# SyncE's order of loads in the opening of a clustered attention and gated feed-forward kernel

## The chip, the cores and the metric

One core of one Trainium2 chip. The metric is the device time of one execution in microseconds (us); 299.18 us is the median of three runs of the kernel before (298.58 to 301.35). SyncE issues most of the transfers, GpSimd the weights' loads and the later values; TensorE, ScalarE, VectorE and GpSimd compute.

## The reference

Attention in which a query sees only the keys of its own cluster, and then a gated feed-forward layer without a gate matrix:

```python
def _attn_ref(q, k, v, centroids):            # q, k, v: (4, 8, 768, 64); centroids: (8, 16, 64)
    q_assign = argmax(einsum('bhsd,hcd->bhsc', q_n, c_n))      # nearest of 16 normalised centroids
    k_assign = argmax(einsum('bhsd,hcd->bhsc', k_n, c_n))
    mask = q_assign[:, :, :, None] == k_assign[:, :, None, :]
    scores = where(mask, scale * q @ k.T, -1e9)
    return softmax(scores) @ v

def _moe_ref(x, w_in, w_out):                 # x: (3072, 512), d_ff 2048
    h = x @ w_in
    return (h * sigmoid(h)) @ w_out
```

## The kernel before

**Jobs.** The rows of queries and keys come in jobs of 128 partitions by up to 12 pieces of 64. Jobs k0 to k7 hold batch 0's keys of one head and the first half of its queries; x0 and x1 hold the second halves of batch 0's queries for four heads each (the extra queries); h8 to h31 hold queries and keys of one head of batches 1 to 3. A job is loaded (`load`), split into a high and a low half in f16 (`hi`, `lo`, lines 123 to 132), transposed (on TensorE with `tr` in the opening, by a DMA transpose, `xpose`, line 141, later), multiplied with the centroids (`psN`, line 180), and the one-hot of the nearest cluster becomes 16 further rows of the transposed tile `ab`, the codes. In the opening `cd_ev` takes the codes out of PSUM and SyncE copies them into `ab` by a small transfer (line 261: "code transfer", 40 or 48 KB). With the codes in the contraction a score of unlike clusters comes out so low that its exponential vanishes.

**Score units.** A unit (`qk`, line 354, then `ex` on ScalarE, line 359) is two key tiles by 384 queries. The first 24 units are the first query halves of batch 0's heads 0 to 7, three units a head: units 0 to 2 need job k0, 3 to 5 k1, 6 to 8 k2, 12 to 14 k4. Each pair of heads then gets its products with the values (`pO`, line 371), is normalised and transposed into `xt`, and the feed-forward units (`ph`, line 421, tanh and gate) and the second matrix (`po`, lines 480 and 561) follow.

**Order.** The scheduling is by hand: an engine runs its instructions in the order in which the program issues them. The opening, up to score unit 26, is written out word by word in `plan`: `vl1` loads the values of head 1, `v1` casts them on GpSimd, `r8` loads job h8 (two transfers of 192 KB, queries and keys), `xr0` loads x0 (one of 384 KB), `xh0` and `xl0` split it, `ce1` to `ce7` take out a job's codes and issue their transfer, `w0` to `w11` load weights from GpSimd. Behind the opening a small planner takes over: each engine has a lane of pieces with the time from which they can run, and picks the one whose due time (ready plus `late`) is first. `load_v` and `cast_v` are the values' load and cast there; five buffers `vn` hold values between load and cast. All that SyncE issues goes in one order, a wait of one transfer holding back those behind it.

Of the kernel before, what the change touches and what calls it, by code (L numbers as in the profile page):

```python
# [34 lines left out]
def kernel(  # L35
# [11 lines left out]
    B, H, S, D = q.shape  # L47
# [240 lines left out]
    def load_v(i, eng=nc.sync):  # L288
        vn = mp.tile([128, NJ, D], f32, name="vn", bufs=5)
        eng.dma_start(vn.rearrange("p j d -> p (j d)"), v[i // H, i % H].rearrange("(p j) d -> p (j d)", j=NJ))  # L290
        vns[i] = vn
# [397 lines left out]
    def first(op, n, eng, banks):  # L689
# [93 lines left out]

    plan = """
        hk0 hq0 hi1.A lk0 cn0 lq0 lo1 tk0.0 hi2.A evk0.D j3.1 c5.12 kad tq0.3 lo2 evq0.A tr1.23 stk vl4 L0.0 vl0
        evq1.A evk1.D mx0 ge0 hi4.A tr2.13 evq2.A L1.2 hi3.P ct0.03 lo4 mx1 ge1 xr0 cm1 ctk0 hi5.P evk2.A lo5 ctq0
        tr4.10 ce1.A qk0 hi7.P evk4.A lo3 L2.3 evq4.A tr5.21 mx2 evk5.D ge2 qk1 ex0 qk2 evq5.A w0 lo7 L4.0 vl1 ex1 mx4
        cm2 tr3.12 ex2 ce2.A xr1 qk3 evq3.D evk3.A qk4 hi6.P tr7.32 ge4 lo6 cm4 L3.1 evq7.D xh0.P ex3 qk5 vl2 evk7.D
        ce4.A v4 mx3 w1 ex4 tr6.20 evk6.D ex5 L5.3 ge3 mx5 vl5 qk6 v1 evq6.A ct3.21 vl3 ge5 qk7 cm5 L6.0 xl0 ctk3 ex6
        ctq3 qk8 ce5.A L7.S.2 xq0.3 mx6 ge6 ls7 xp0.1 xw0.D v0 xh1.P w2 ex7 cm6 v2 v5 qk9 ex8 ce6.A qk10 ex9 pa0.3 mx7  # L790
        ge7 pb0 vl6 xu0.D xl1 qk11 xL0.0 ex10 cm7 vl7 qk12 v3 ex11 xM0 ce7.D xs0 w3 pc0 v7 qk13 r8 xp1.1 ex12 qk14 xm0
        ex13 xu1.D ex14 w4 xq1.2 qk15 xg0 v6 nm0 pa1.1 qk16 xw1.D xc0 pt0.3 ex15 xe0.D ex16 qk17 ex17 xL1.2 w5 pb1
        qk18 vl8 ex18 xM1 qk19 pe0.D pc1 qk20 nm1 vl9 xs1 pa2.0 ex19 ex20 qk21 pb2 qk22 ex21 pc2 xm1 xg1 ex22 nm2 w6
        qk23 px3.3 pt1.1 pe1.D ex23 pt2.0 xc1 py3 qk24 pe2.D w7 r9 xe1.A r10 nm3 ex24 qk25 a0.1 pt3.0 w8 qk26 a1.2
# [38 lines left out]
    def lands(t, work, rest):  # L833
        nonlocal moves_end
        moves_end = max(t, moves_end) + work
        return moves_end + rest

    def add(eng, ready, length, f, then=None, late=0.0):
        lanes[eng].append((ready, ready + late, length, f, then))
# [120 lines left out]
    def value_free(i, t):  # L960
        if i - 5 not in cast_at:
            after_cast[i - 5] = lambda t: value_free(i, t)
            return
        t = max(t, cast_at[i - 5] + 0.06)
        if i >= 2 * H:
            add("POOL", t, 0.6, lambda: load_v(i, nc.gpsimd), lambda t: got_v(i, t))
        else:
            add("SP", t, 0.7, lambda: load_v(i), lambda t: got_v(i, t))

    def got_v(i, t):  # L970
        values_at[i] = lands(t, 0.78, 1.0)
        if i in waiting:
            waiting.pop(i)(t)
# [18 lines left out]
    for i in range(H, B * H):  # L992
        b, h = divmod(i, H)
        p = SPLIT[i - H]
        job = jobs[i]
        if i > H + 3:
            date(p - AHEAD[b - 1], lambda t, i=i: raw_free(i, t))
        if i >= H + 2:
            date(p - VALUES[b - 1], lambda t, i=i: value_free(i, t))
        date(p, chain(job, b))  # L1000
        date(p + CAST[b - 1], lambda t, i=i: cast(i, t))
# [305 lines left out]
    while True:  # L1307
# [11 lines left out]
        t, e, piece = best  # L1319
# [34 lines left out]
```

## Time and profile before

| | |
|---|---|
| median of 3 runs | 299.18 us (298.58 to 301.35) |
| profiled execution | 297.6 us, its span 295.8 us |
| TensorE busy | 288.1 us of the span (97%) |
| ScalarE, VectorE, GpSimd busy | 222.0, 219.3, 73.4 us |
| granted TensorE clock | 0.999 |
| transfers | 44.61 MB, mean 151 GB/s |

The times in the views are in us from the start of the span. A line such as "19.60 0.81 ACT L359" gives start, length, engine and the line of the kernel; in square brackets stands how long the engine had been idle before it, and what ended that. A line "ab<-cd SPq DMA_DIRECT2D x1, 40.0 KB, 3.9" is a transfer issued by SyncE, its size and the time from issue to landing. PE is TensorE, PEld its loading of weights, ACT ScalarE, DVE VectorE, POOL GpSimd, SP SyncE.

### The profile page before, as it was taken

To read this page: it belongs to the slowest core of one execution; us is meant where nothing else is said; L and a number is where in the kernel's file an instruction comes from. 1 tells how busy PE (TensorE), PEld (TensorE's weight loads), DVE (VectorE), ACT (ScalarE), POOL (GpSimd) and SP (SyncE) were. 2 spreads that over 40 slices of the span, in tenths; PEclk is the share of its full clock that TensorE was granted. 3 is DMA by queue.
4 is the path that set the end of the run, shared out by engine and by line. 5 is a ranking of instruction groups with operands and counts; after the bars stand their busy time and mean duration, and the time that the engine had idled before them with its cause. 6 is when DMAs were issued, how large, how long until landed. Compare 5 with 4: busy or idle time off the path is not lost.

```text
span 295.8 us, 8187 instructions
## 1 busy us (share of the span) xinstructions
PE 288.1 (97%) x3273; PEld 203.5 (69%) x3273; DVE 219.3 (74%) x459; ACT 222.0 (75%) x365; POOL 73.4 (25%) x133
## 2 busy tenths in 40 slices
PE   7899999999999999999999999999999999999995
PEld 3777766666765566667766776778767786767783
DVE  5999679496997799997797676997664644569743
ACT  5899889655896679987579668997798879744410
POOL 2985700002050023652332540252300000000000
PEclk9999999999999999999999999999999999999999
DMA  7888999999866499989987979796210020110013
GB/s 216 249 175 187 204 256 196 182 264 204 233 139 182 110 227 224 230 195 206 219 174 147 188 218 228 175 122 126 73 50 17 13 86 16 49 38 0 35 38 142
DMA packets 77220, 44.61 MB, mean 151 GB/s; under 512 B 56288, under 2 KB 73088, under 8 KB 77184
## 3 DMA queue, kind: packets, MB, share of 16 engines
q1 hardware_dynamic: 71952, 35.55, 52.0%
q0 software_dynamic: 4800, 8.13, 14.6%
q8 instruction: 25, 0.41, 0.6%
q10 hardware_dynamic: 432, 0.43, 0.4%
q14 instruction: 11, 0.09, 0.1%
HBM read 27.30 MB, written 6.29 MB: 114 GB/s over the span
## 4 chain that ended last, share of the span: by engine, by line
PE 87%; DMA 5%; ACT 4%; DVE 2%; issue 1%; DVEq 0%; ACTq 0%
PE ph L421 28%; PE pS L354 19%; PE po L561 16%; PE pO L371 10%; PE po L480 8%; PE psN L180 3%; ACT P L359 3%; DMA ab<-hl 2%; DMA ab<-cdt 1%; DVE hl L132 1%; DMA ab<-cd 1%; DMA raw<-in_k_dram 1%; ACT ab L164 0%; PE px L393 0%; PE psC L246 0%
## 5 line engine op out<-in xcount | busy, mean ns | idle before, releaser
L359 ACT ACTIVATE P<-pS 128x768 f16<-128x768 f32 x192 | 156.6, 825 | 34.9 <-PE pS L354 33.9
L421 PE MATMUL ph<-xt,win_s 128*128 128x384 f16 x512 | 97.6, 326 | 0.0
L354 PE MATMUL pS<-ab 128*128 128x384 f16 x384 | 93.3, 326 | 1.0 <-DMA ab<-cd 0.5
L444 DVE SCALAR_TENSOR_TENSOR gt<-tn,ph 128x384 f16<-128x384 f32 x110 | 58.6, 550 | 21.2 <-ACT tn L441 20.5
L421 PEld LDWEIGHTS <-win_s 128*128 128x128 f16 x512 | 49.2, 98 | 31.2
L441 ACT ACTIVATE tn<-ph 128x384 f32<-128x384 f32 x110 | 55.2, 514 | 3.2 <-PE ph L421 2.3
L354 PEld LDWEIGHTS <-ab 128*128 128x128 f16 x384 | 34.4, 98 | 19.7 <-DMA ab<-cd 0.9
L371 PEld LDWEIGHTS <-P 128*128 128x128 f16 x1152 | 39.8, 97 | 4.4
L371 PE MATMUL pO<-vt,P 128*128 128x65 f16 x1152 | 41.2, 193 | 0.0
L561 PEld LDWEIGHTS <-gt 128*128 128x128 f16 x304 | 29.3, 98 | 6.0 <-DVE gt L544 0.4
L132 DVE SCALAR_TENSOR_TENSOR hl<-raw,hl 128x768 f16<-128x768 f32 (+3 forms) x35 | 32.4, 931 | 0.6 <-ACT hl L123 0.3
L480 PE MATMUL po<-wout_s,gt 128*128 128x512 f16 x128 | 32.5, 379 | 0.0
L295 POOL CAST vt<-vn 128x384 f16<-128x384 f32 x32 | 19.2, 607 | 50.7 <-DMA vn<-in_v_dram 38.1
L561 PE MATMUL po<-wout_s,gt 128*128 128x256 f16 x192 | 24.4, 273 | 0.0
L224 POOL TENSOR_SCALAR od<-od 128x96 f16<-128x96 f16 x16 | 10.0, 627 | 57.3 <-DVE od L217 57.2
L180 PEld LDWEIGHTS <-ab 128*128 128x128 f16 x458 | 17.4, 97 | 4.7 <-DMA ab<-hl 0.8
L381 DVE RECIPROCAL zr<-pO 128x6 f32<-128x6 f32 x32 | 6.2, 193 | 19.1 <-PE pO L371 19.0
L480 PEld LDWEIGHTS <-gt 128*128 128x128 f16 x128 | 12.0, 98 | 10.7
L180 PE MATMUL psN<-stk,ab 128*128 128x32 f16 (+1 forms) x458 | 18.6, 188 | 0.6 <-DMA ab<-hl 0.6
L383 DVE TENSOR_TENSOR xn<-pO,zr 128x384 f16<-128x384 f32 x32 | 17.8, 557 | 1.1
L192 DVE TENSOR_REDUCE L<-psN 128x192 f32<-128x384 f32 (+1 forms) x27 | 14.8, 549 | 2.3 <-PE psN L180 2.2
L561 PE MATMUL po<-tw,sg 128*128 128x256 f16 x128 | 16.3, 273 | 0.0
(101 smaller groups left out, 259.1 us busy)
## 6 DMA issues: line engine op xcount, KB each, us to landing
raw<-in_k_dram SPq DMA_DIRECT2D x31, 192.0 KB, 3.8
out_dram<-ot SPq DMA_DIRECT2D x23, 256.0 KB, 2.3
raw<-in_q_dram SPq DMA_DIRECT2D x24, 192.0 KB, 4.1
vn<-in_v_dram SPq DMA_DIRECT2D x16, 192.0 KB, 4.0
vn<-in_v_dram POOLq DMA_DIRECT2D x16, 192.0 KB, 3.5
win_s<-in_moe_w_in_dram POOLq DMA_DIRECT2D x8, 256.0 KB, 6.1
wout_s<-in_moe_w_out_dram POOLq DMA_DIRECT2D x4, 512.0 KB, 19.5
raw<-in_q_dram SPq DMA_DIRECT2D x2, 384.0 KB, 4.7
```

The source lines that it names most:

```text
L132: nc.vector.scalar_tensor_tensor(out=hl[:, s, 1, :], in0=raws[job.name][:, s, :], scalar=QS, in1=hl[:, s, 0, :], op0=ALU.mult, op1=ALU.sub ...
L180: nc.tensor.matmul(L[:, n % g, :, n // g], ab[:, i, :], stk[:, job.groups[i // 3][0], x : x + w], start=(x == 0), stop=(x + w == 2 * HC),)
L295: nc.gpsimd.tensor_copy(vt[:, :, 0:D], vns.pop(i))
L354: nc.tensor.matmul(pS[:, e, 0:HALF], abs_[kj.name][:, kn, :], rhs, start=True, stop=True)
L359: nc.scalar.activation(out=P, in_=pst.pop(u)[:, :, 0:HALF], func=AF.Exp, bias=0.0, scale=ESC)
L371: nc.tensor.matmul(o[:, (2 * t + h) * VW : (2 * t + h + 1) * VW], Ps[i + h, c, j // 2][:, j % 2, ts(t, 128)], vtb[(i + h) % 13][:, j, 0:VW ...
L383: nc.vector.tensor_tensor(out=xn, in0=ov[:, :, 0:D], in1=zr.unsqueeze(2).to_broadcast([128, 2 * NM, D]), op=ALU.mult)
L421: nc.tensor.matmul(ph[:, 0:HALF], win_s[:, r, ts(fb, 128)], xts[b, c][:, r, :], start=(r == 0), stop=(r == NR - 1))
L441: nc.scalar.activation(out=tn, in_=ph[:, 0:HALF], func=AF.Tanh, bias=0.0, scale=1.0)
L444: nc.vector.scalar_tensor_tensor(out=gt[:, fb, :], in0=tn, scalar=1.0, in1=ph[:, 0:HALF], op0=ALU.add, op1=ALU.mult)
L480: nc.tensor.matmul(po, gts[b, c][:, fc, ts(t, 128)], wout_s[:, fc, :], start=(fc == 0), stop=(fc == NFB - 1))
L561: nc.tensor.matmul(o, l[:, f, :], x, start=(f == 0 and k in begins), stop=(f == HK - 1), skip_group_check=True)
```

## The change

Two words of `plan` move, and one argument in the planner. `xr0` moves from ahead of `cm1` to behind `ce1`; `r8` moves from behind `qk13` to behind `vl1`; and a load of values by SyncE for heads 8 to 11 gets 3 us more until it is due.

```diff
-        evq1.A evk1.D mx0 ge0 hi4.A tr2.13 evq2.A L1.2 hi3.P ct0.03 lo4 mx1 ge1 xr0 cm1 ctk0 hi5.P evk2.A lo5 ctq0
-        tr4.10 ce1.A qk0 hi7.P evk4.A lo3 L2.3 evq4.A tr5.21 mx2 evk5.D ge2 qk1 ex0 qk2 evq5.A w0 lo7 L4.0 vl1 ex1 mx4
+        evq1.A evk1.D mx0 ge0 hi4.A tr2.13 evq2.A L1.2 hi3.P ct0.03 lo4 mx1 ge1 cm1 ctk0 hi5.P evk2.A lo5 ctq0
+        tr4.10 ce1.A xr0 qk0 hi7.P evk4.A lo3 L2.3 evq4.A tr5.21 mx2 evk5.D ge2 qk1 ex0 qk2 evq5.A w0 lo7 L4.0 vl1 r8 ex1 mx4
...
-        ge7 pb0 vl6 xu0.D xl1 qk11 xL0.0 ex10 cm7 vl7 qk12 v3 ex11 xM0 ce7.D xs0 w3 pc0 v7 qk13 r8 xp1.1 ex12 qk14 xm0
+        ge7 pb0 vl6 xu0.D xl1 qk11 xL0.0 ex10 cm7 vl7 qk12 v3 ex11 xM0 ce7.D xs0 w3 pc0 v7 qk13 xp1.1 ex12 qk14 xm0
...
-            add("SP", t, 0.7, lambda: load_v(i), lambda t: got_v(i, t))
+            add("SP", t, 0.7, lambda: load_v(i), lambda t: got_v(i, t), 3.0 if i < H + 4 else 0.0)
```

The order of the instructions differs on SyncE alone. In the opening, from behind the last loads of batch 0's rows (`vn` are values; `raw` of 128x4x192 the extra queries, of 128x384 h8's rows; `ab<-cd` the code transfers of k1, k2, k4, k5 and k6), before:

```order
L290 DMA vn<-in_v_dram 128x384 x2
L113 DMA raw<-in_q_dram 128x4x192
L261 DMA ab<-cd 16x5x256
L290 DMA vn<-in_v_dram 128x384
L261 DMA ab<-cd 16x5x256
L113 DMA raw<-in_q_dram 128x4x192
L290 DMA vn<-in_v_dram 128x384
L261 DMA ab<-cd 16x5x256
L290 DMA vn<-in_v_dram 128x384 x2
L261 DMA ab<-cd 16x5x256 x2
L290 DMA vn<-in_v_dram 128x384 x2
L261 DMA ab<-cd 16x5x256
```

and now:

```order
L290 DMA vn<-in_v_dram 128x384 x2
L261 DMA ab<-cd 16x5x256
L113 DMA raw<-in_q_dram 128x4x192
L290 DMA vn<-in_v_dram 128x384
L111 DMA raw<-in_q_dram 128x384
L111 DMA raw<-in_k_dram 128x384
L261 DMA ab<-cd 16x5x256
L113 DMA raw<-in_q_dram 128x4x192
L290 DMA vn<-in_v_dram 128x384
L261 DMA ab<-cd 16x5x256
L290 DMA vn<-in_v_dram 128x384 x2
L261 DMA ab<-cd 16x5x256 x2
```

The first code transfer stands ahead of the first extra queries now, and between it and the second code transfer stand one load of 384 KB, one of 192 KB (the values of head 1) and the two of h8, where only the values stood.

In the planned part, at the DMA transpose of job h11, the piece that differs:

```order
-L290 DMA vn<-in_v_dram 128x384 x2
+L290 DMA vn<-in_v_dram 128x384
 L141 DMA_TRANSPOSE ab<-hl 128x12x128
-L261 DMA ab<-cd 16x6x256 x2
+L261 DMA ab<-cd 16x6x256
+L290 DMA vn<-in_v_dram 128x384
+L261 DMA ab<-cd 16x6x256
```

Of the two loads of values ahead of the transpose (heads 11 and 12), head 11's now stands behind the transpose and behind h8's code transfer.

## The prediction

> **What bounds the kernel now.** I read the page first: the span, the engines' shares, the chain.
>
> ```profile
> span 295.8 us, 8187 instructions
> PE 288.1 (97%) x3273; PEld 203.5 (69%) x3273; DVE 219.3 (74%) x459; ACT 222.0 (75%) x365; POOL 73.4 (25%) x133
> DMA  7888999999866499989987979796210020110013
> PE 87%; DMA 5%; ACT 4%; DVE 2%; issue 1%; DVEq 0%; ACTq 0%
> ```
>
> TensorE is busy for 288.1 of 295.8 us. The edit moves nothing but transfers, so it can move the end only where TensorE waits, and in the stretch before TensorE is the limit. The DMA row says that the transfers are dense in the first 70 us, but a slice of 7.4 us is too coarse for the opening. So next the busy time by stretches of 5 us:
>
> ```profile
> core 0: us, PE busy (x) PEld busy (x) DVE busy (x) ACT busy (x) POOL busy (x), PEclk, DMA share, GB/s
> 5.00:10.00 5.00, 4.31 (x76) 3.15 (x73) 4.83 (x13) 3.69 (x9) 2.57 (x2) 1.00 1.01 311
> 15.00:20.00 5.00, 4.40 (x80) 3.42 (x77) 4.37 (x12) 4.79 (x9) 4.43 (x6) 1.00 0.76 183
> 20.00:25.00 5.00, 5.00 (x94) 3.87 (x92) 4.87 (x11) 4.95 (x9) 3.83 (x4) 1.00 0.85 172
> 30.00:35.00 5.00, 4.77 (x102) 3.98 (x101) 3.45 (x9) 4.62 (x7) 4.17 (x9) 1.00 0.97 193
> 60.00:65.00 5.00, 4.41 (x60) 2.84 (x57) 4.44 (x11) 2.18 (x4) 0.50 (x1) 1.00 1.08 243
> ```
>
> From 15 to 35 us ScalarE has no room (4.79, 4.95 and 4.62 of 5 us): a score unit that comes late there is late at the end of the opening. Between 35 and 60 us TensorE's rows read 5.00 of 5.00. The next hole after the opening is 0.59 us in 60 to 65. The DMA engines have slack at 15 to 20 (share 0.76) and none at 30 to 35 and 60 to 65 (0.97 and 1.08). The chain of waits, in order of time, names what lies at the two places:
>
> ```profile
> 15.76 3.26 DMA ab<-cd
> 19.07 0.50 PE pS L354 x2
> 36.94 4.71 PE ph L421 x29
> 57.51 5.48 DMA ab<-hl
> 63.03 0.52 PE psN L180 x12
> 87.91 1.09 PE pO L371 x36
> ```
>
> The first is the second code transfer (job k2's codes, `ce2` in the plan), asked for at 15.76 and waited for by score unit 6 at 19.07. The second is the transpose of job h10's rows. The timeline shows how tight the first is:
>
> ```profile
> 8.84 0.39 SPq L113 DMA_DIRECT2D raw<-in_q_dram  x1
> 11.85 0.72 SPq L261 DMA_DIRECT2D ab<-cd  x1
> 12.62 0.57 SPq L290 DMA_DIRECT2D vn<-in_v_dram  x1
> 15.76 0.59 SPq L261 DMA_DIRECT2D ab<-cd  x1
> 16.40 0.58 SPq L113 DMA_DIRECT2D raw<-in_q_dram  x1
> 17.78 0.57 SPq L261 DMA_DIRECT2D ab<-cd  x1
> 15.80 0.82 PE L354 MATMUL pS<-ab 128*128 128x384 f16 x4 [0.54 <-DMA ab<-cd]
> 19.06 0.11 PEld L354 LDWEIGHTS <-ab 128*128 128x128 f16 x2 [0.15 <-DMA ab<-cd]
> 19.60 0.81 ACT L359 ACTIVATE P<-pS 128x768 f16<-128x768 f32 x1
> ```
>
> Unit 6 starts the moment k2's codes land (0.15 us of waiting), and its exponential on ScalarE follows at 19.60. Whatever that transfer loses, the opening loses. For each transfer, the issues with their time to landing (the first code transfer at 11.85, the second at 15.76, the third at 17.78, the second group of extra queries at 16.40, h8's queries at 26.24):
>
> ```profile
> ab<-cd SPq DMA_DIRECT2D x1, 40.0 KB, 3.9
> ab<-cd SPq DMA_DIRECT2D x1, 40.0 KB, 3.3
> ab<-cd SPq DMA_DIRECT2D x1, 40.0 KB, 5.8
> raw<-in_q_dram SPq DMA_DIRECT2D x1, 384.0 KB, 3.8
> raw<-in_q_dram SPq DMA_DIRECT2D x1, 192.0 KB, 5.9
> ```
>
> **The change part by part.** Nothing is added or removed. On SyncE (1) `xr0` goes from 8.84 to behind the first code transfer, so to 11.85 + 0.72 = about 12.6; (2) h8's two loads go from 26.24 to behind the third load of values, where they end at about 12.6 + 5 x 0.5 = 14.7 at the latest (xr0 0.6, v1 0.5, h8 2 x 0.45, gaps); (3) in the planned part the values of head 11 go behind a transpose and a code transfer. The other four engines keep their order.
>
> *First code transfer.* It is still issued at 11.85, when ScalarE hands over the codes, now without 384 KB asked for ahead of it. Bounds: 3.9 us as now, 3.3 us as the second one with little ahead of it, so 0 to 0.6 us sooner. TensorE waits 0.54 us for it at 15.80. I put the gain at 0, because unit 6 comes next and waits for the second code transfer whatever happens here.
>
> *Second code transfer.* Its issue at 15.76 also waits for ScalarE, and SyncE is through with h8's loads 1 us before, so the issue isn't late. What is late is the data: ahead of it on the same queue stand 384 + 192 + 384 = 960 KB since 12.6, where 192 KB stood, and 256 KB of weights from GpSimd are under way too. Below: 3.3 us as now, landing at 19.06, loss 0 (a gain is at most the 0.15 us of waiting). Above: the third transfer, which had 576 KB ahead of it on this queue and 256 KB of weights beside, took 5.8 us; with that the second lands at 21.56, 2.5 us late. Between them by the same row read another way: the third landed at 17.78 + 5.8 = 23.58, which is 7.2 us after the first of the 576 KB was asked for at 16.40. The same 7.2 us from 12.6 give 19.8; the 384 KB more would add 0.393 MB at 311 GB/s = 1.3 us, but the queue has 3.2 us rather than 1.4 us to work before the codes are asked for, so I leave that out. I take 19.85, a **loss of 0.8 us**. It passes whole to 36.94, where TensorE takes over, since ScalarE has no gap to make it up.
>
> The Trainium skill speaks to this in "DMA: Bandwidth & Descriptors", "Queues, rings and completion order": on each DMA engine the descriptors of one issuing engine's row are consumed in ring order, so the codes can't pass the loads. That is against the change, and the 5.8 us row agrees with it. By the same page's fabric ceiling of 435 GB/s, though, 960 KB would be an estimated 2.3 us of work, done before the codes are asked for, and the loss would be 0. None of the 5 us stretches above shows more than 311 GB/s, so the sum goes by the rows.
>
> *Extra queries later.* They are scaled on GpSimd, then on VectorE.
>
> ```profile
> 13.66 3.88 POOL L125 TENSOR_SCALAR hl<-raw 128x576 f16<-128x576 f32 x2
> 20.32 2.29 POOL L125 TENSOR_SCALAR hl<-raw 128x768 f16<-128x768 f32 x1 [0.81 <-DMA raw<-in_q_dram]
> 19.67 0.95 DVE L132 SCALAR_TENSOR_TENSOR hl<-raw,hl 128x768 f16<-128x768 f32 x1
> 42.69 1.02 DVE L127 TENSOR_SCALAR hl<-raw 128x768 f16<-128x768 f32 x2
> ```
>
> The 3.88 us are h6's split and then x0's (2.29 by its twin), so x0 starts at about 15.3 and ends at 17.54. Asked for at 12.6, its rows land at 16.4 (3.8 us, as the other group's) and it ends at 18.7, ahead of VectorE at 19.67. What stands behind it on GpSimd (casts of v4, v1, v0 and the second weight load) slides by 1.1 us and is caught at 20.32, where GpSimd waits 0.81 us now. Cost 0; were the rows to land after 17.4 us, VectorE would wait.
>
> *h8 sooner.* Its consumer is VectorE at 42.69, and it lands at 26.24 + 5.9 = 32.1 already: nothing at the consumer. But 384 KB leave a full queue: 0.393 MB at 311 to 193 GB/s is 1.3 to 2.0 us of queue time. The queue is full until the transposes, where it is paid back:
>
> ```profile
> 63.03 0.26 PE L180 MATMUL psN<-stk,ab 128*128 128x32 f16 x3 [0.59 <-DMA ab<-hl]
> 63.11 0.87 SPq L290 DMA_DIRECT2D vn<-in_v_dram  x2
> 64.09 1.94 SPq L141 DMA_TRANSPOSE ab<-hl  x1
> 66.55 1.28 SPq L261 DMA_DIRECT2D ab<-cd  x2
> ab<-hl SPq DMA_TRANSPOSE x1, 5.5
> ab<-hl SPq DMA_TRANSPOSE x8, 4.9
> ```
>
> h10's transpose takes 5.5 us behind h9's; the median of the eight in the first 100 us is 4.9. At 4.9 it saves 0.6 us, the whole wait of 0.59. Bounds: 0 (its time is its own) to 0.59 (TensorE has no more hole there). I take a **gain of 0.6 us**, the queue being shorter by more than that.
>
> *Values of head 11 later.* At 63.11 SyncE issues two loads in 0.87 us, afterwards one: the transpose at 64.09 and the first code transfer at 66.55 come 0.4 us sooner. TensorE waits for neither now, so 0. The values come after about 66.5 + 4 = 70.5; they are read by the products of batch 1's heads 2 and 3, the sixth group of 36 in the planned part, at 87.91, 17 us on. Cost 0, cover 17 us.
>
> *Sum.* Against the profiled execution of 297.6 us (its span 295.8 and 1.8 around it): 297.6 + 0.8 - 0.6 = 297.8. The median of the three runs, 299.18, is 1.58 us above that execution, so **299.4 us**.
>
> **The rivals.**
>
> *The codes stick behind the loads (slower).* The second code transfer pays the third's 5.8 us: 2.5 us lost on ScalarE's path, 0.6 us given back: 299.18 + 1.9 = 301.1 us. It decides from a landing later than about 20.7, where the loss outgrows gain and noise. For it: the 5.8 us row. Against: the loads have 1.8 us more of a start. From 22.7 us on (7 us to landing) it is over 1%.
>
> *Only the relief counts (faster).* The dip (0.76 at 15 to 20 us) swallows 768 KB, the second code transfer still lands by 19.1, and the first lands 0.6 us sooner: 299.18 - 0.6 = 298.6, at best another 0.5 us from the 0.54 us wait, 298.1. For it: unit 6 waits only 0.15 us. Against: 192 KB ahead became 960 KB.
>
> *GpSimd slides (slower).* x0's rows land as late as 18.2, its split ends at 20.5, VectorE is 0.8 us late at 19.67 and the casts behind push the first products: at most 1.5 us, 300.7. Against it: 1 us of cover.
>
> *It does nothing.* The code transfers set SyncE's times (each issue waits for codes), and the wait of 0.59 us is the transpose's own: 299.2.
>
> **How the numbers follow.** The forecast, no change worth the name (298.7 to 300.3), with the case that it does nothing: 0.5. Codes stick: 0.27. Only the relief: 0.17. GpSimd: 0.06. The range that leaves out 2 in 10 reaches from 298.0 (the relief) to 301.7 (the codes at 5.8 us with a little noise). 1%, 3 us, is about what a measurement of this kernel can tell from no change. Faster by that needs more waiting taken away than the 0.59 + 0.54 + 0.15 us that is there: 0.03. Slower by that needs the codes at 7 us: about a third of that rival, 0.10. Within: 0.87.
>
> **What would show it.** Right: a wait of 0.5 to 1.2 us for the second code transfer before score unit 6, the wait at 63 us gone, time to landing of the first code transfer at 3.3 to 3.9. Wrong: no wait at unit 6 (then faster), or ScalarE idle for over 2 us between 18 and 23 us (then slower); a VectorE wait for GpSimd at 19.7 would name the third rival, and a wait at 63 us of 0.5 us or more the end of the relief.

## The result and the profile after

The changed kernel takes 301.89 us in the median of 19 runs (299.68 to 303.90), the kernel before 298.58 us beside it (19 runs): a ratio of 1.0092, 95% interval 1.0069 to 1.0115. It is 0.9% slower, 2.8 us of span in the profiled executions (298.6 against 295.8). The page of the changed kernel, its span, busy times and chain:

```profile
span 298.6 us, 8186 instructions
PE 289.4 (97%) x3273; PEld 205.3 (69%) x3273; DVE 219.5 (74%) x459; ACT 221.8 (74%) x365; POOL 72.6 (24%) x133
PE 88%; DMA 5%; ACT 4%; DVE 1%; issue 1%; SPq 0%; ACTq 0%
```

The shares tell nothing; the loss is in one place. The busy time of the changed kernel by stretches (columns as before: TensorE, its loading, VectorE, ScalarE, GpSimd, granted clock, DMA share, GB/s):

```profile
15.00:20.00 5.00, 3.63 (x70) 2.94 (x67) 4.35 (x13) 4.31 (x8) 4.00 (x5) 1.00 1.06 298
20.00:25.00 5.00, 3.87 (x53) 2.99 (x54) 1.98 (x6) 3.26 (x5) 3.85 (x4) 0.75 0.80 196
25.00:30.00 5.00, 5.00 (x81) 4.16 (x80) 4.42 (x10) 3.77 (x6) 1.90 (x5) 0.91 0.71 101
60.00:65.00 5.00, 5.00 (x78) 3.42 (x77) 3.51 (x8) 3.18 (x4) 0.51 (x1) 1.00 1.23 182
```

Between 20 and 25 us ScalarE has fallen from 4.95 to 3.26 of 5 us, TensorE from 5.00 to 3.87, and a column moved that had stood at 1.00: the granted clock is 0.75, then 0.91. The hole at 60 to 65 us has closed. By single microseconds:

```profile
19.00:20.00 1.00, 0.00 (x0) 0.00 (x0) 0.97 (x3) 0.31 (x1) 0.99 (x3) 1.00 1.11 316
20.00:21.00 1.00, 0.00 (x0) 0.00 (x0) 0.40 (x1) 0.00 (x0) 1.00 (x2) 1.00 1.31 307
21.00:22.00 1.00, 0.87 (x10) 0.56 (x11) 0.00 (x0) 0.34 (x1) 0.21 (x1) 1.00 0.98 233
22.00:23.00 1.00, 1.00 (x17) 0.77 (x15) 0.62 (x2) 0.95 (x2) 0.65 (x1) 0.74 1.00 244
24.00:25.00 1.00, 1.00 (x17) 1.00 (x16) 0.51 (x2) 0.97 (x2) 1.00 (x2) 0.50 0.24 66
25.00:26.00 1.00, 1.00 (x12) 1.00 (x11) 0.85 (x3) 0.00 (x0) 0.99 (x4) 0.55 0.13 13
26.00:27.00 1.00, 1.00 (x20) 0.74 (x18) 0.96 (x3) 0.82 (x2) 0.91 (x2) 1.00 0.97 150
```

TensorE does nothing from 19 to 21 us. It goes on at 21.1, and 1.3 us later it is given half its clock, from about 22.5 to 25.9 us. What it waited for, in the timeline (transfers issued by SyncE, then the waits of TensorE and ScalarE, then the extra queries on GpSimd and VectorE):

```profile
11.91 0.72 SPq L261 DMA_DIRECT2D ab<-cd  x1
12.68 0.58 SPq L113 DMA_DIRECT2D raw<-in_q_dram  x1
13.30 0.50 SPq L290 DMA_DIRECT2D vn<-in_v_dram  x1
13.85 0.43 SPq L111 DMA_DIRECT2D raw<-in_q_dram  x1
14.33 0.44 SPq L111 DMA_DIRECT2D raw<-in_k_dram  x1
15.81 0.59 SPq L261 DMA_DIRECT2D ab<-cd  x1
21.13 0.50 PE L354 MATMUL pS<-ab 128*128 128x384 f16 x2 [2.42 <-DMA ab<-cd]
21.66 0.81 ACT L359 ACTIVATE P<-pS 128x768 f16<-128x768 f32 x1 [2.35 <-PE pS L354]
16.37 2.23 POOL L125 TENSOR_SCALAR hl<-raw 128x768 f16<-128x768 f32 x1 [0.99 <-DMA raw<-in_q_dram]
19.37 1.03 DVE L132 SCALAR_TENSOR_TENSOR hl<-raw,hl 128x768 f16<-128x768 f32 x1
```

And the times to landing in the changed kernel: the first code transfer, h8's keys, the second code transfer.

```profile
ab<-cd SPq DMA_DIRECT2D x1, 40.0 KB, 2.3
raw<-in_k_dram SPq DMA_DIRECT2D x1, 192.0 KB, 5.7
ab<-cd SPq DMA_DIRECT2D x1, 40.0 KB, 5.3
```

SyncE issues the second code transfer at 15.81, as before. h8's keys land at 14.33 + 5.7 = 20.0, and the codes behind them at 15.81 + 5.3 = 21.1. Score unit 6 starts at 21.13 where it started at 19.07. The chain of the changed kernel gives the rest of the account:

```profile
15.81 5.27 DMA ab<-cd
21.13 0.50 PE pS L354 x2
40.33 4.71 PE ph L421 x29
```

The opening's end is 40.33 - 36.94 = 3.4 us late: 2.06 us from the codes, and 1.33 us between unit 6 and that point, where the same work took longer, 3.4 us of it at half the clock. At the end 2.8 us are left, so 0.6 us came back on the way.

### The profile page after: what moved, and what is told of

Its sections match the earlier page's. It is cut to its first block, busy times and chain, and to the rows that moved or that the text cites. A ratio compares the mean times of both kernels' runs of the same rounds, so it can differ in the third digit from the quotient of the medians.

```text
span 298.6 us, 8186 instructions
## 1 busy us (share of the span) xinstructions
PE 289.4 (97%) x3273; PEld 205.3 (69%) x3273; DVE 219.5 (74%) x459; ACT 221.8 (74%) x365; POOL 72.6 (24%) x133
## 4 chain that ended last, share of the span: by engine, by line
PE 88%; DMA 5%; ACT 4%; DVE 1%; issue 1%; SPq 0%; ACTq 0%
PE ph L421 28%; PE pS L354 19%; PE po L561 16%; PE pO L371 11%; PE po L480 9%; PE psN L180 3%; ACT P L359 3%; DMA ab<-cd 2%; DMA ab<-cdt 1%; DMA raw<-in_q_dram 1%; DVE hl L132 1%; PE px L393 1%; ACT ab L164 0%; PE psC L246 0%; DVE ab L166 0%
## 5 line engine op out<-in xcount | busy, mean ns | idle before, releaser
L444 DVE SCALAR_TENSOR_TENSOR gt<-tn,ph 128x384 f16<-128x384 f32 x110 | 58.6, 548 | 21.1 <-ACT tn L441 20.4
L354 PEld LDWEIGHTS <-ab 128*128 128x128 f16 x384 | 34.6, 98 | 21.8 <-DMA ab<-cd 2.5
L132 DVE SCALAR_TENSOR_TENSOR hl<-raw,hl 128x768 f16<-128x768 f32 (+3 forms) x35 | 31.7, 909 | 0.7 <-ACT hl L123 0.3
L180 PEld LDWEIGHTS <-ab 128*128 128x128 f16 x458 | 17.8, 98 | 4.1 <-issue 0.3
## 6 DMA issues: line engine op xcount, KB each, us to landing
wout_s<-in_moe_w_out_dram POOLq DMA_DIRECT2D x4, 512.0 KB, 17.3
```

Source lines behind the costliest of these rows:

```text
L132: nc.vector.scalar_tensor_tensor(out=hl[:, s, 1, :], in0=raws[job.name][:, s, :], scalar=QS, in1=hl[:, s, 0, :], op0=ALU.mult, op1=ALU.sub ...
L180: nc.tensor.matmul(L[:, n % g, :, n // g], ab[:, i, :], stk[:, job.groups[i // 3][0], x : x + w], start=(x == 0), stop=(x + w == 2 * HC),)
L354: nc.tensor.matmul(pS[:, e, 0:HALF], abs_[kj.name][:, kn, :], rhs, start=True, stop=True)
L444: nc.vector.scalar_tensor_tensor(out=gt[:, fb, :], in0=tn, scalar=1.0, in1=ph[:, 0:HALF], op0=ALU.add, op1=ALU.mult)
```

## The experiments

Theory A: the codes stick behind the loads, and the wait lets the clock drop. Its main rivals: the late extra queries do it (B), the clock drop has nothing to do with the wait (C), or h8's loads do harm by themselves (D, and G wherever they stand). All ratios are to the kernel before, run on the same chip beside them; its median there was 298.94 us beside e1 to e4, 298.82 beside e5 to e8 and 299.02 beside e9 and e10. A ratio is not the quotient of two medians. e6 and e10 have 8 executions, the other runs 12, the changed kernel 19. The last two columns are of the one profiled execution.

| run | what moved | median us | ratio (95%) | second codes, us to landing | wait at unit 6, us |
|---|---|---|---|---|---|
| changed kernel | all | 301.89 | 1.0092 (1.0069 to 1.0115) | 5.3 | 2.42 |
| e1 | extra queries alone | 298.40 | 0.9986 (0.9961 to 1.0012) | 2.9 | none |
| e2 | h8 alone | 299.29 | 1.0013 (0.9987 to 1.0040) | 3.6 | 0.72 |
| e3 | head 11's values alone | 298.31 | 0.9977 (0.9951 to 1.0003) | 2.7 | none |
| e4 | all, wait filled | 300.59 | 1.0072 (1.0041 to 1.0103) | 5.1 | filled |
| e5 | all, but only half of h8 | 299.06 | 1.0045 (1.0013 to 1.0077) | 4.0 | 1.17 |
| e6 | all, h8 behind the second codes | 301.23 | 1.0086 (1.0053 to 1.0119) | 3.2 | 0.40 |
| e7 | all, h8 behind the third codes | 298.94 | 1.0024 (1.0002 to 1.0045) | 3.9 | 1.03 |
| e8 | all but h8 | 298.90 | 1.0006 (0.9978 to 1.0033) | 3.5 | 0.66 |
| e9 | head 1's and head 11's values | 298.47 | 0.9987 (0.9966 to 1.0008) | 2.6 | none |
| e10 | all, wait half filled | 301.06 | 1.0088 (1.0054 to 1.0123) | 4.6 | 0.50 |

### Each part alone

```diff
e1: - ge1 xr0 cm1          + ge1 cm1 ... ce1.A xr0 qk0
e2: - qk13 r8 xp1.1        + vl1 r8 ex1 ... qk13 xp1.1
e3: - lambda t: got_v(i, t))    + lambda t: got_v(i, t), 3.0 if i < H + 4 else 0.0)
```

> Only the extra queries' first load moves behind the first code transfer; h8's loads and head 11's values stay as before. Theory A (the second code transfer sticks behind the loads put ahead of it, and the wait it causes lets the TensorE clock drop): with 576 KB ahead instead of 960 the second code transfer lands at 19.0 to 19.6, TensorE waits 0 to 0.6 us for it, the granted clock stays at 1.00 between 20 and 30 us, and the time is within 0.5 us of before (299 us). Rival B (the loss comes from the extra queries being late on GpSimd and VectorE): most of the 2.8 us are lost here too, about 301 us. Rival C (the clock drop is chance and not tied to the wait): the clock between 20 and 30 us may drop here as well.

> Only h8's two loads move behind the third load of values; the extra queries keep their early place. Theory A: 576 KB (values 192, h8 384) stand ahead of the second code transfer, h8's k rows land at about 18, the code transfer at 18.5 to 19.6; TensorE waits 0 to 0.6 us, the clock stays at 1.00, and the relief after 26 us is kept, so the wait of 0.59 us near 63 us is gone: 298.2 to 299.2 us, 0 to 0.6 us faster than before. Rival B: as before or better, since the extra queries are not late. Rival D (h8's early load alone does the harm whatever else is ahead): a wait of about 2 us and 301 us.

> Only head 11's values are issued behind the transpose and the code transfer. Theory A: nothing waits for these sooner, within 0.3 us of before. Rival E (part of the loss is in the planned part, from these values): 0.5 us or more slower, with a wait of the products at 88 us or of GpSimd's cast that holds others.

None of the three is distinguishable from the kernel before. Rival B falls with e1: the extra queries are as late there as in the changed kernel and nothing is lost. Rival D falls with e2: h8's loads alone, in their new place, leave a wait of 0.72 us at unit 6 and no measurable loss at the end. Its lines of the issues and of the timeline:

```profile
ab<-cd SPq DMA_DIRECT2D x1, 40.0 KB, 3.6
19.69 0.50 PE L354 MATMUL pS<-ab 128*128 128x384 f16 x2 [0.72 <-DMA ab<-cd]
```

It takes both moves together. Either alone puts 576 KB ahead of the second codes, and that costs at most 0.72 us of waiting here; 960 KB cost 2.42.

### Between 576 and 960 KB

e5 puts h8's keys back to their old place and leaves the queries early.

```diff
- vl1 r8 ex1 ... qk13 xp1.1
+ vl1 rq8 ex1 ... qk13 rk8 xp1.1        # rq: queries, rk: keys of the same load
```

> The changed kernel with h8's keys (192 KB) back at their old place and its queries (192 KB) early: 768 KB instead of 960 ahead of the second code transfer. Theory A (it waits for its turn in the queue): it lands about halfway between 19.1 (576 KB) and 21.1 (960 KB), at 20.0 to 20.4; TensorE waits 1.0 to 1.5 us. If a gap of that length is too short for the clock to drop, it stays at 1.00 and the time is 0.6 to 1.2 us above before, 299.5 to 300.2; if it drops, 300.5 to 301. Rival F (the number of transfers, or the pair of h8's loads together, makes the delay, not the bytes): it lands at 19.1 or at 21.1.

```profile
ab<-cd SPq DMA_DIRECT2D x1, 40.0 KB, 4.0
20.12 0.50 PE L354 MATMUL pS<-ab 128*128 128x384 f16 x2 [1.17 <-DMA ab<-cd]
```

The codes land at 16.05 + 4.0 = 20.1, between the two, and the kernel's ratio (1.0045) lies between theirs, though its median hardly differs from that beside it (299.06 against 298.82). So what stands ahead in the queue counts, and the pair of h8's loads is not needed for a delay. Whether it is the bytes or the number of loads isn't shown, since the two rise together here (one load for 192 KB, two or three for 576, three for 768, four for 960). The time to landing goes 2.6 (nothing ahead of it since the first codes, e9), 2.7 and 3.3 (192 KB: e3, before), 2.9 to 3.9 (576: e1, e2, e6, e7, e8), 4.0 (768), 4.6 to 5.3 (960: the changed kernel, e4, e10). The spread of one amount is up to 1.0 us, so a size is known to no better than that. In this profile the granted clock stayed at 1.00 after the wait of 1.17 us.

### The wait filled

```diff
- vl5 qk6 v1
+ vl5 j10.2 qk6 v1        # e4: ten matmuls of 512 columns on the zero tile; e10: j5.2, five
```

> The changed kernel with ten matmuls of 512 columns on a zero tile put into TensorE's order just ahead of score unit 6, where it waits (about 2.2 us of work that nothing reads). Theory A: they fill the wait of 2.4 us, the granted clock stays at 1.00 between 20 and 26 us, score unit 6 still starts at about 21.1, and the time is 1.2 to 1.5 us below the changed kernel's (about 300.5 against 301.9), the rest of the loss being the late codes. Rival C (the clock drop is not caused by the wait): the clock is 0.5 for some 3.4 us as without them and the time stays at 301.9 or rises. If the wait alone were the loss and the clock cost nothing: 301.9.

The timeline and the stretches of e4:

```profile
19.01 2.32 PE L625 MATMUL junk<-zz 128*128 128x512 f16 x10
21.25 0.50 PE L354 MATMUL pS<-ab 128*128 128x384 f16 x2
20.00:25.00 5.00, 5.00 (x70) 3.33 (x68) 2.77 (x8) 3.16 (x6) 3.78 (x5) 1.00 0.91 230
25.00:30.00 5.00, 5.00 (x88) 3.71 (x87) 4.90 (x12) 4.94 (x8) 2.33 (x5) 1.00 0.79 161
```

Unit 6 starts at about the same time as in the changed kernel, 21.25 against 21.13, and the clock stays at 1.00 in both stretches. That holds for all executions: in each of the 12 of e4 the mean granted clock was 0.998 or more, while in 16 of the 19 of the changed kernel it was 0.994 or less. So rival C falls: the codes were as late as before, and with TensorE at work in the gap the drop was gone.

What the drop costs is less sure. From unit 6 to unit 24 (the first of the extra queries') the changed kernel takes 17.3 us, e4 16.1, the kernel before 15.9. e4 is 1.3 us below the changed kernel in the medians, as theory A said, and 0.8 us in the spans of the profiled executions. By the ratios it is 0.2%, some 0.6 us, and their intervals overlap. The three executions of the changed kernel with a clock of 0.998 or more had spans of 297.9, 298.2 and 300.8 us, the other sixteen 297.9 to 302.1, so the clock is not all that moves the time from one execution to the next.

> The changed kernel with five zero matmuls of 512 columns (about 1.1 us of work that nothing reads) ahead of score unit 6, half of what filled the wait. TensorE then waits 1.0 to 1.4 us in one piece. If a gap of that length does not let the clock drop (the kernel with half of h8 early waited 1.2 us at a clock of 1.00), the clock stays at 1.00 and the time is that of the ten matmuls, 300.3 to 300.9. If the idle time counts in total or any gap over 1 us drops the clock, 301.5 to 302.

This one came out between and does not settle the price. In its profile the codes happened to land at 4.6 us, only 0.50 us of waiting was left behind the five matmuls, and the clock stayed at 1.00; in none of its eight executions was the mean clock under 0.997. Yet its median (301.06) lies between e4's and the changed kernel's, and its ratio (1.0088) is hardly below the changed kernel's. How long a gap must be to cost the clock: 1.17 us in e5 and 1.53 us in e6 (below) were not enough in those profiles, 2.42 us were. Where between 1.53 and 2.42 us the border lies, and whether the length alone decides, is open: one execution of e5 had a mean clock of 0.994, with no profile to tell its gap.

### h8 behind the codes

```diff
e6: - vl1 r8 ex1    + vl1 ex1 ... ce2.A r8 xr1
e7: - vl1 r8 ex1    + vl1 ex1 ... ce4.A r8 v4
e8: no move of r8
```

> The changed kernel with h8's two loads one place later, behind the second code transfer and ahead of the second group of extra queries. Theory A: the second code transfer lands at 19.0 to 19.3 without a wait; the next victim is the third code transfer, now behind 384 KB more: it lands at 24 to 25.5 rather than 23, against a need at about 24.7, so TensorE waits 0 to 0.8 us at score unit 12, the clock stays at 1.00, 298.5 to 300. Rival G (h8's rows anywhere in the opening cost the 2 to 3 us, by contention with all that moves): about 301.

> The changed kernel with h8's two loads behind the third code transfer, some 8 us earlier than before the change and behind every code transfer that TensorE waits for. Theory A: no wait for codes, the clock stays at 1.00; what is left is the relief of the full queue from 26 us on. If that is worth what the prediction took, the time is 0.6 us below before, and below the kernel without h8's move (next run); if the relief is worth nothing, it equals that one within 0.3 us.

> The extra queries behind the first code transfer and head 11's values behind the transpose, h8's loads at their old place: the change without its costly part. Each alone came out 0.1 to 0.2% below before, inside its interval. Expected 0 to 0.4% below before (297.8 to 299).

e6 was a surprise. Unit 6 waits 0.40 us and unit 12 not at all, as theory A had it, but the kernel is as slow as rival G said, at a clock of 1.00 in the profile. The stall is further on, at unit 24. Its timeline, the stretch around it, and two issues beside it (a weight load that GpSimd asked for at 29.9 us, and the code transfer of the first extra queries, asked for at 30.1):

```profile
37.89 0.81 PE L354 MATMUL pS<-ab 128*128 128x384 f16 x4 [1.53 <-DMA ab<-cd]
35.00:40.00 5.00, 3.47 (x53) 2.56 (x50) 2.02 (x6) 2.60 (x5) 1.84 (x4) 1.00 1.09 234
win_s<-in_moe_w_in_dram POOLq DMA_DIRECT2D x1, 256.0 KB, 8.1
ab<-cd SPq DMA_DIRECT2D x1, 48.0 KB, 7.7
```

The extra queries' codes were 7.7 us under way beside GpSimd's weights, where before the change they took 5.9 and landed 0.3 us ahead of need. Ahead of that stall e6 is already 1.2 us late (unit 18 starts at 30.41 us, before the change at 29.22), made up of small waits. That stall was not tried by an edit, but the twelve traces point at the weights: from 29 us on, later in some runs, GpSimd asks for them in a close series, and what differs is when that series starts. In e6 it started 1.2 us ahead of the code transfer, which took 7.7 us. In the kernel before, e2, e8 and e9 it started within a quarter of a microsecond of it, and the codes took 4.9 to 6.0 us. In e1 it started 0.8 us behind, and they took 4.1. In the other six traces it started more than 1 us behind, and they took 2.2 to 3.5 us, in e7 2.7. Other loads differ too between these runs, so this is an order that fits and not a proof.

e7, behind the third codes, has no such stall, and rival G falls with it; but it is still no faster than e8, which leaves h8 alone: 1.0024 against 1.0006, intervals overlapping. Theory A's "no wait for codes" did not hold in e7 either: unit 6 waited 1.03 us there with 576 KB ahead of its codes, and 0.66 us in e8. The relief of the full queue is worth nothing that can be measured.

### Nothing ahead of the second codes

```diff
- vl1 ex1 mx4 cm2 tr3.12 ex2 ce2.A xr1
+ ex1 mx4 cm2 tr3.12 ex2 ce2.A vl1 xr1        # and head 11's values late, on the kernel before
```

> The kernel before with nothing of the loads ahead of the second code transfer: the values of head 1 move behind it, and head 11's values behind the transpose, all else as before. Theory A (what stands ahead of the second code transfer on SyncE's queue sets its landing): it lands 2.9 to 3.3 us after its issue, TensorE waits 0 to 0.15 us at score unit 6; its price lies in head 1's cast on GpSimd, which has 4 us of cover. 0 to 0.4% below before (297.6 to 298.8). If it is slower, the order of the other transfers behind it matters as much.

The second codes land in 2.6 us, the fastest of all, and unit 6 doesn't wait. The ratio is 0.9987, interval 0.9966 to 1.0008: no change. The wait of 0.15 us was all there was to win at this place. No version here beats the kernel before clear of noise.

## Why the prediction was right or wrong

**The place was right, the size was not.** The forecast was no change worth the name, 299.4 us, with a loss of 0.8 us at the second code transfer. The measured ratio, 1.0092, lies inside 1% but at its upper end, and it is clear of noise; the measured 301.89 us lie just above the range of 298.0 to 301.7. It is what the rival "the codes stick behind the loads" forecast in sign and place (its mark was a landing later than 20.7 us, and the codes landed at 21.1), with the price from the third transfer's row (5.8 us; 5.3 measured) nearer than the one chosen (4.1).

**The step that failed first** is the term "second code transfer", 0.8 us where 2.06 were measured. Between the bounds it took the 7.2 us reading of the third transfer's row and then left out the 384 KB more, because the queue had 3.2 us rather than 1.4 us to work. That start was no gain: the 7.2 us are counted from the first asking, so it is in them already, and the transfers began late in both kernels (before the change the DMA share was 0.46 and 0.47 from 16 to 18 us, behind the asking at 16.40). These are the microseconds after SyncE had asked for the first of the 960 KB, at 12.68 us in the changed kernel:

```profile
12.00:13.00 1.00, 1.00 (x29) 0.92 (x27) 1.00 (x2) 1.00 (x3) 1.00 (x2) 1.00 0.00 0
13.00:14.00 1.00, 0.93 (x10) 0.54 (x8) 0.97 (x4) 1.00 (x3) 0.97 (x2) 1.00 0.29 49
14.00:15.00 1.00, 1.00 (x31) 0.97 (x29) 1.00 (x4) 1.00 (x3) 1.00 (x1) 1.00 0.70 159
```

From 12 to 13 us the DMA engines stood idle, and they were not full before 15 us (share 0.00, 0.29, 0.70); before the change the extra queries asked for at 8.84 us were still moving there (0.71 in 12 to 13 us). With the 1.3 us that the prediction worked out and left out, its sum gives 19.8 + 1.3 = 21.1 us, and the codes landed at 21.08; the spread of 4.6 to 5.3 us at this amount makes the close hit partly luck. e5 says the same with less: from 768 to 960 KB the codes lost 0.6 to 1.3 us, where 192 KB at 311 GB/s are 0.6 us. By the Trainium skill, "DMA: Bandwidth & Descriptors", "Queues, rings and completion order", the descriptors of a row are consumed in ring order; h8's keys landing at 20.0 and the codes at 21.1 agree. The estimate from the 435 GB/s of that page of the Trainium skill, no loss, does not hold: the stretch 15 to 20 us moved 298 GB/s at a DMA share of 1.06.

**What was missing** is the clock. The prediction had ScalarE pass the delay on one to one; it had no term for what TensorE pays after standing still. In the profiled executions that is 1.33 us more, and 2.06 + 1.33 - 0.6 gives the 2.8 us of the spans; over all executions its size is only known to lie about 0.6 to 1.3 us, the difference between e4 and the changed kernel by ratios and by medians. The Trainium skill, "TensorE: Matmul & The Clock Gate", "Part 1: The HAM clock gate (the "warmup" mystery)", says that the clock falls to half after an idle window of about 3.4 us and that the window runs free; the length of the drop here, 3.4 us from 22.5 to 25.9, agrees. The Trainium skill's advice on the same page, in "Why this matters for your kernels", is to have no gaps over about 3 us, so it would not have given the drop: here 2.42 us sufficed.

**The gain of 0.6 us came, but not from where it was put.** The hole at 60 to 65 us closed in the changed kernel (4.41 to 5.00): TensorE was 3.3 us late at the piece ahead of it (63.89 us against 60.57) and 2.6 us late behind it (65.63 against 63.03). The hole also closed in e1 and e3, in which h8's loads are at their old place. Their stretches, e1 first:

```profile
60.00:65.00 5.00, 4.92 (x91) 3.64 (x90) 4.32 (x11) 2.77 (x4) 0.51 (x1) 1.00 1.05 272
60.00:65.00 5.00, 4.96 (x91) 3.59 (x90) 4.90 (x12) 2.90 (x4) 0.51 (x1) 1.00 1.10 242
```

Both reach that place over a microsecond late, for the most part because TensorE waits for weights just ahead of 45 us (1.11 us in e1, 0.81 in e3):

```profile
44.09 0.34 PE L421 MATMUL ph<-xt,win_s 128*128 128x384 f16 x1 [1.11 <-DMA win_s<-in_moe_w_in_dram]
```

So TensorE arrives late, at about the time when the transpose lands: the hole is slack that any delay up to 0.6 us uses up, not a gain of the relief. e2, with h8's loads early, shows it most plainly. Its unit 6 was 0.6 us late (19.69 us against 19.07), and behind the hole it is level again:

```profile
63.01 0.52 PE L180 MATMUL psN<-stk,ab 128*128 128x32 f16 x12
ab<-hl SPq DMA_TRANSPOSE x1, 5.5
```

h10's transpose took 5.5 us there as before the change, and 5.2 in the changed kernel, where the prediction had 4.9. In none of the other eleven traces is the hole over 0.23 us, not even in e3, whose order up to 63 us is that of the kernel before: the 0.59 us were those of one execution, and the closed hole, which the prediction took for a sign of being right, tells nothing. The step "h8 sooner" was right in the sum by luck; the transposes, and e7 against e8, show it wrong in its reason.

**The first code transfer** landed in 2.3 us, 1 us below the lower bound of 3.3. The wait of 0.54 us went, and as said it bought nothing, since unit 6 was next. That moving the extra queries made it faster isn't shown: in e2, which leaves them ahead of it, it took 2.3 us too.

**GpSimd** did what was worked out: the extra queries' split started at 16.37 (16.4 forecast), ended at 18.6, and VectorE followed at 19.37 without waiting. Head 11's values cost nothing that can be measured (e3).

**The signs to look for** named it: ScalarE idle for over 2 us between 18 and 23 us (2.35) was the sign of slower.

## What to carry to other kernels

A small transfer that an engine is waiting for should not be issued behind large loads that nobody needs yet, and it is all that stands ahead together that counts: two moves that were each free within the noise (576 KB) cost 2.8 us together (960 KB). A head start of a queue is worth only what the transfers move in it. When a stall is to be priced on TensorE, ask how long it stands still: a stall of 2.4 us here was followed by half the clock, and paid for a second time in part, where stalls up to 1.5 us were not. And a hole further down the line is not a gain waiting to be taken; it may be just the slack that swallows the next delay.

## What the runs showed of the hardware

A gap of 2.42 us in TensorE's work was followed, 1.3 us after it went on, by a granted clock of 0.50 for 3.4 us; gaps of 1.17 us (e5) and 1.53 us (e6) were not, and ten matmuls on zeros in the gap kept it at 1.00 (e4: a mean clock of 0.998 or more in all 12 executions, against 0.994 or less in 16 of 19). The second code transfer, of 40 KB, took 2.6 us with nothing asked for by SyncE since the one before it and 4.6 to 5.3 us behind 960 KB. One of 48 KB took 7.7 us where a series of GpSimd's weight loads had started 1.2 us ahead of it, and 2.2 to 3.5 us where that series started more than 1 us behind it.
